# Unpacking of two 64-bit weights and placement of small copies in a fused attention, mixture and SoLU kernel

## The chip, the cores and the metric

The kernel runs on one core of one Trainium2 chip. The metric is the device time of one execution in microseconds. The engines of the core are TensorE (PE in the profile), VectorE (DVE), ScalarE (ACT), GpSimd (POOL) and SyncE (SP, which here only issues DMAs). Each engine works through its own instructions strictly in the order in which they stand; between engines they wait for semaphores.

## The reference

Three layers follow each other; what matters here is the last two.

```python
p_packed = sm_attn(p, k, v)              # 8 batches, 8 heads, 576 positions, 64 wide, 32 packed
x = sm_attn(q, p_packed, p_packed)       # -> x of 4608 x 512
logits = x @ phi                         # 32 slots = 8 experts x 4
d = softmax over tokens;  slot_input = d.T @ x
for e in range(8):
    h = np.maximum(slot_input[e] @ w1[e], 0.0)     # 512 -> 1024
    slot_out[e] = h @ w2[e]                        # 1024 -> 512
x = (softmax over slots) @ slot_out
h = x @ w_in                             # 512 -> 1024
solu = h * softmax(h);  ln = (solu - mean) / sqrt(var + 1e-6) * g_ln
out = ln @ w_out                         # 1024 -> 512
```

`w_in` and `w_out` arrive as 64-bit floats (a 32-bit array times a 64-bit scalar). [...]

## The kernel before

It has three stages on the chip, and a planner that orders the first two together and the third by itself.

**Stage 1, attention and routing (0 to about 128 us).** Eight batches in four pairs; K, Q, V are loaded into a ring of 14 tiles (`ring`, tile `r`). For each pair the packed attention, its softmax (tiles `A`, `bmx`, `bsum`), the transposes and the running softmax over tokens are made. Between these the planner puts the unpacking of `w_in` (tile `wif`), marked `soft`: only into gaps. Stage 1 ends with the slot inputs `SIT`.

**Stage 2, the experts (about 128 to 192 us).** The weights of the eight experts come in 29 loads of 9 pieces (`w12`) through the same ring. For expert e, `mk_w1` multiplies 16 pieces with `SIT` (L935), takes the ReLU into `hs` on ScalarE (L946), transposes it on TensorE (L951) and copies it out as `hT` (L955); `mk_w2` multiplies 16 pieces with `hT` (L976), copies the result to `so` on ScalarE (L991), transposes it (L995) and writes it, scaled and three times, into `SO` (L1000). A copy `hs` or `so` thus stands between two pieces of TensorE work. `sw` = `SO` x `w_in` (L1214) ends the stage.

Beside the experts `w_out` is unpacked in eight chunks of 128x512 (`mk_unpack`, with `wo_bound` and `wo_tail`):

- VectorE takes the exponent bits of the upper word into `ux` (L1077) and the mantissa bits into `ua` (L1080); ScalarE turns the exponent into that of a 32-bit float, in place in `ux` (L1087, a ReLU with the bias `ebias`).
- TensorE multiplies the power of two in `ux`, read as 16-bit numbers two apart, with `ga` and adds it up over the eight chunks (`wo_bound`, L1141): a bound from which the column scales `wsc` and `winv` come.
- VectorE adds the lower word to the mantissa (L1092) and, after the bound's multiplication has read `ux`, puts the sign bit onto `ux` (L1099). GpSimd multiplies `ua` by `ux` (L1152).

When all eight are done, ScalarE copies the bound (L1161), VectorE makes the scales in four steps (L1165 to L1178), and then for each chunk VectorE scales it (`q1`, L1188), ScalarE rounds it to 16 bits as `whi` (`q2`, L1193) and GpSimd subtracts this to get `wlo` (`q3`, L1196).

**Stage 3 (about 201 us to the end).** 36 tiles of 128 tokens: `h` (L1272), softmax and norm on VectorE, ScalarE and GpSimd, then 24 multiplications of 128x512 a tile with `whi` and `wlo` (L1392, L1398). In its steady part TensorE follows itself without a gap.

**What sets the order.** `Plan` lists each step with its engine, an estimated length, what it depends on, buffers it takes (`acq`) and gives back (`rel`) and an urgency, plays this through, and writes the instructions in the order of the start times that come out. Estimates only decide the order; on the chip an engine waits at its next instruction, whatever stands behind it. Idle places of TensorE are filled with multiplications of zeros (`wz`, L319).

Of the kernel before, what the change touches and what calls it, by code (L numbers as in the profile page):

```python
# [138 lines left out]
def pack_attention__soft_moe__solu_kernel(  # L139
# [55 lines left out]
    with ExitStack() as p12, tc.manual_schedule():  # L195
# [12 lines left out]

        phi_sb = at.tile([128, 4, 32], FP32, name="phi_sb", bufs=1)
        plan = Plan({"ring": RING, "ring2": 0, "sc": 2, "w": 4, "v": 0, "a": 4, "aT": 2, "grp": 5, "ST": 1, "A2": 2, "A2T": 1, "d": 1, "T": 1,  # L210
                     "h": 2, "u": 2, "c3": 1}, LOOK1, CALM1, REST1)
        now = [0]

        def op(*args, urgent=0, **kw):
# [712 lines left out]
        def mk_w1(e):  # L927
            def pe(g0, g1):
                def go():
                    if g0 == first(e):  # L930
                        ps_t["h", e] = bank()
                    hp = ps_t["h", e]
                    for i in range(g0, g1):
                        k, g = divmod(i - first(e), 4)
                        nc.tensor.matmul(  # L935
                            out=hp[32 * g:32 * g + 32, 0:256],
                            lhsT=SIT[:, k, :],
                            rhs=gran(i),
                            start=(k == 0),
                            stop=(k == 3),  # L940
                        )
                return go

            def act():
                hs = hs_t[e] = W["k"].tile([128, 256], FP32, tag="hs", name="hs")
                nc.scalar.activation(out=hs, in_=ps_t.pop(("h", e))[:, 0:256], func=ACTF.Relu)  # L946

            def tr():
                t = ps_t["ht", e] = bank()
                for j in range(2):  # L950
                    nc.tensor.transpose(t[:, 128 * j:128 * j + 128], hs_t[e][:, 128 * j:128 * j + 128], ident)  # L951

            def dve():
                hT = hT_t[e] = W["k"].tile([128, 2, 4, 32], FP32, tag="hT", name="hT")
                nc.vector.tensor_copy(  # L955
                    hT, ps_t.pop(("ht", e))[:, 0:256].rearrange("p (j g s) -> p j g s", j=2, g=4)
                )

            x = stream(first(e), first(e) + 16, pe, 95, [o_2, o_w1.get(e - 1)], ["w", "h"], [])
            o_w1[e] = x  # L960
            x = op("ACT", 264, act, [x], rel=["w"])
            x = op("PE", 214, tr, [x], acq=["w"])
            o_hT[e] = op("ACT" if 0 else "DVE", 330, dve, [x], rel=["w"], urgent=10 ** 5)

        def mk_w2(e):
            def pe(g0, g1):
# [18 lines left out]
            def tail(h0, h1, dep):  # L985
# [11 lines left out]
                def dve():  # L997
# [12 lines left out]
            s0, s1 = second(e), second(e) + 16  # L1010
            o = [o_hT[e], o_w2.get(e - 1)]
# [52 lines left out]
        def mk_unpack(key, c, tail, deps, between=None):  # L1064
            def words():
                raw = loaded[key][:, 1024 * c:1024 * c + 1024].bitcast(UINT32).rearrange("p (n w) -> p n w", w=2)
                return raw[:, :, 0], raw[:, :, 1]

            def dve():
                lo, hi = words()  # L1070
                if key[0] == "wi":
                    a = wif[:, key[1], 512 * c:512 * c + 512]
                else:
                    a = W["k"].tile([128, 512], FP32, tag="ua", name="ua")
                ua_t[key, c] = a
# [29 lines left out]
            x = op("DVE", ns[0], dve, deps, acq=["u"], soft=so)  # L1105
            y = op("ACT", ns[1], act, [x], soft=so)
            z = op("DVE", ns[2], dve2, [x], soft=so)
            ys = [y, between(2 * key[1] + c, key, c, y)] if between else [y]
            z = op("DVE", ns[3], dve3, ys + [z], rel=["ring"] if key[0] == "wi" and c == 1 else [], soft=so)
            return tail(key, c, z)  # L1110

        def wi_tail(key, c, z):
            def pool():
                a, x = ua_t.pop((key, c)), ux_t.pop((key, c))
                nc.gpsimd.tensor_tensor(out=a, in0=a, in1=x.bitcast(FP32), op=ALU.mult)

            return op("Pool", 1225, pool, [z], rel=["u"], soft=True)

# [18 lines left out]
        def wo_bound(k, key, c, dep):  # L1137
            def pe():
                if k == 0:
                    ps_t["bd"] = bank2()  # L1140
                nc.tensor.matmul(  # L1141
                    out=ps_t["bd"], lhsT=W["ga"][:, k, :], rhs=ux_t[key, c].bitcast(BF16).rearrange("p (n w) -> p n w", w=2)[:, :, 1],
                    start=(k == 0), stop=(k == 7),
                )

            o_bd.append(op("PE", 220, pe, [dep, o_ga] + o_bd[-1:], acq=["v"] if k == 0 else [], urgent=10 ** 5))
            return o_bd[-1]

# [37 lines left out]
        for k in range(8):  # L1186
# [11 lines left out]
            y = op("DVE", 1100, q1, [x, o_wo[k]])  # L1198
# [355 lines left out]
```

## Time and profile before

| | us |
|---|---|
| three runs | 417.67, 419.58, 419.73 |
| median | 419.58 |
| the profiled execution | 419.56 |
| its span | 417.7 |
| busy in it: PE, DVE, ACT, POOL | 393.2, 280.3, 231.5, 197.6 |

A row of the profile gives start or busy time, engine, line of the kernel, the tile that is written and those that are read, shape and count. In brackets stands the idle time of the engine before the row and what ended it. A multiplication of 32-bit floats on TensorE stands as two records.

### The profile page before, as it was taken

How to read it: one execution, taken by the hardware profiler on the slowest of the kernel's cores; microseconds unless marked ns; L12 is line 12 of the kernel's file. 1: busy time of each engine (PE TensorE's matmuls, PEld its weight loads, DVE VectorE, ACT ScalarE, POOL GpSimd, SP SyncE). 2: the span in 40 equal slices, each digit the busy share in tenths (PEclk: the TensorE clock that was granted, in tenths of full speed). 3: DMA queues.
4: the chain of work that ended last, by engine and by line, in shares of the span. 5: the costliest groups of instructions: out<-in, count | busy, mean ns of one | idle time of the engine just before them, and what ended most of it. 6: DMA issues, size and time to landing. Idle time of an engine off the chain costs nothing.

```text
span 417.7 us, 9713 instructions
## 1 busy us (share of the span) xinstructions
PE 393.2 (94%) x3807; PEld 210.6 (50%) x3807; DVE 280.3 (67%) x587; ACT 231.5 (55%) x430; POOL 197.6 (47%) x296
## 2 busy tenths in 40 slices
PE   8989999998799999879879999999999999999997
PEld 3455565655445777544334444444444444444445
DVE  2177889988956465880896666667666767766641
ACT  1357777867444334240588556665566556666530
POOL 1033545351610222291179665666665666656650
PEclk9999999999999999998999999999999999999999
DMA  8999999999999999900037756776756867668662
GB/s 305 414 418 407 416 412 414 415 418 412 417 423 376 391 375 423 385 4 0 0 52 168 171 117 126 140 163 137 136 121 136 154 137 127 146 124 148 151 142 86
DMA packets 91149, 99.27 MB, mean 238 GB/s; under 512 B 76128, under 2 KB 76640, under 8 KB 85472
## 3 DMA queue, kind: packets, MB, share of 16 engines
q1 hardware_dynamic: 90816, 98.58, 73.9%
q8 instruction: 30, 0.49, 0.5%
q14 instruction: 15, 0.12, 0.1%
q10 hardware_dynamic: 288, 0.07, 0.1%
HBM read 70.85 MB, written 9.44 MB: 192 GB/s over the span
## 4 chain that ended last, share of the span: by engine, by line
PE 74%; DVE 13%; DMA 7%; issue 2%; ACT 2%; POOL 1%; SPq 1%; ACTq 0%; DVEq 0%; POOLq 0%
PE o L1392 28%; PE o L1398 14%; PE w L976 5%; PE w L935 4%; PE h L1272 3%; DMA r<-kT 3%; DMA r<-qT 3%; PE sc L335 2%; DVE r L1188 2%; PE w L418 2%; PE sw L1214 2%; PE w L319 2%; DVE bmx L507 2%; PE w L575 1%; PE o L1405 1%
## 5 line engine op out<-in xcount | busy, mean ns | idle before, releaser
L1392 PE MATMUL o<-whi,th 128*128 128x512 f16 x280 | 106.1, 379 | 1.7 <-DMA th<-hi 1.3
L1392 PE MATMUL o<-wlo,th 128*128 128x512 f16 x280 | 106.1, 379 | 0.0
L1362 POOL TENSOR_TENSOR lo<-x,hi 128x1024 f16<-128x1024 f32 (+1 forms) x37 | 77.4, 2093 | 29.5 <-ACT hi L1355 29.5
L1392 PEld LDWEIGHTS <-th 128*128 128x128 f16 x560 | 54.6, 98 | 67.7 <-DMA th<-hi 1.7
L1398 PE MATMUL o<-whi,tl 128*128 128x512 f16 x280 | 66.5, 380 | 0.0
L1321 ACT ACTIVATE e<-s3t,nv 128x1024 f32<-128x1024 f32 x36 | 41.3, 1148 | 43.9 <-DVE nmean L1315 43.9
L1355 ACT ACTIVATE hi<-s3t,nr,rs 128x1024 f16<-128x1024 f32 (+1 forms) x37 | 44.9, 1217 | 25.4 <-POOL nr L1342 25.4
L1302 DVE SCALAR_TENSOR_TENSOR s3t<-h,e 128x1024 f32<-128x1024 f32 (+1 forms) x37 | 44.0, 1191 | 20.2 <-ACT e L1293 20.2
L1347 DVE TENSOR_SCALAR x<-s3t,nmean,rs 128x1024 f32<-128x1024 f32 (+1 forms) x37 | 30.1, 816 | 35.6 <-POOL rs L1338 35.6
L1280 DVE TENSOR_REDUCE nm<-h 128x1 f32<-128x1024 f32 (+1 forms) x37 | 43.9, 1188 | 2.5 <-PE h L1272 2.4
L1398 PEld LDWEIGHTS <-tl 128*128 128x128 f16 x280 | 24.9, 98 | 34.3 <-issue 8.6
L1293 ACT ACTIVATE e<-h,nm 128x1024 f32<-128x1024 f32 (+1 forms) x37 | 39.7, 1074 | 3.4 <-DVE nm L1285 2.9
L976 PE MATMUL w<-r,hT 128*32 128x128 f32 x512 | 30.8, 284 | 0.2 <-DVE hT L955 0.2
L319 PE MATMUL w<-wz 128*128 128x512 f16 x105 | 29.5, 380 | 1.6 <-ACT bq L446 0.5
L1272 PE MATMUL h<-swr,cT 96*128 96x512 f32 x72 | 28.7, 483 | 1.6 <-DVE swr L1226 1.4
L1152 POOL TENSOR_TENSOR r<-ua,ux 128x512 f32<-128x512 f32 x8 | 10.7, 1336 | 38.3 <-DVE ux L1099 38.3
L1420 DVE TENSOR_TENSOR ob<-o,winv 128x512 f32<-128x512 f32 x35 | 24.0, 684 | 5.8 <-PE o L1398 5.8
L976 PEld LDWEIGHTS w<-r,hT 128*32 128x32 f32 x512 | 25.7, 113 | 4.0 <-issue 1.9
L539 POOL TENSOR_TENSOR A<-A,bsum 128x512 f32<-128x512 f32 (+1 forms) x18 | 19.0, 1061 | 18.5 <-DVE bsum L531 11.6
L935 PE MATMUL w<-r,SIT 128*32 128x256 f32 x256 | 22.6, 384 | 0.0
L1338 POOL TENSOR_TENSOR rs<-rs,half 128x1 f32<-128x1 f32 x36 | 20.1, 558 | 2.8
L1337 POOL TENSOR_TENSOR rs<-V,w 128x1 f32<-128x1 f32 x36 | 7.4, 206 | 27.9 <-ACT e L1321 27.9
(187 smaller groups left out, 614.9 us busy)
## 6 DMA issues: line engine op xcount, KB each, us to landing
r<-w SPq DMA_DIRECT2D x28, 1152.0 KB, 11.2
r<-kT SPq DMA_DIRECT2D x16, 576.0 KB, 13.4
r<-v SPq DMA_DIRECT2D x8, 1152.0 KB, 14.1
r<-qT SPq DMA_DIRECT2D x16, 576.0 KB, 14.7
out<-ob SPq DMA_DIRECT2D x31, 256.0 KB, 2.3
r<-w_in SPq DMA_DIRECT2D x4, 1024.0 KB, 14.2
r<-w_out SPq DMA_DIRECT2D x4, 1024.0 KB, 20.5
out<-ob SPq DMA_DIRECT2D x16, 64.0 KB, 1.7
```

The lines of the kernel that those rows point to most:

```text
L319: nc.tensor.matmul(out=t[:, 0:FN], lhsT=wz[:, 0:128], rhs=wz[:, 0:FN], start=True, stop=True)
L935: nc.tensor.matmul(out=hp[32 * g:32 * g + 32, 0:256], lhsT=SIT[:, k, :], rhs=gran(i), start=(k == 0), stop=(k == 3),)
L976: nc.tensor.matmul(out=sp[32 * k:32 * k + 32, 0:128], lhsT=hT_t[e][:, j, g, :], rhs=gran(i)[:, 128 * c:128 * c + 128], start=(f == 0), sto ...
L1272: nc.tensor.matmul(out=w, lhsT=cT[:, t, :], rhs=swr[n], start=True, stop=True)
L1280: nc.vector.tensor_reduce(out=z["nm"][:, h:h + 1], in_=hcols(h), axis=AX.X, op=ALU.max, negate=True)
L1293: nc.scalar.activation(out=z["e"][:, cols(h)], in_=hcols(h), func=ACTF.Exp, bias=z["nm"][:, 0:1], accum_out=z["S"][:, h:h + 1],)
L1302: nc.vector.scalar_tensor_tensor(out=z["s"][:, cols(h)], in0=hcols(h), scalar=1.0, in1=z["e"][:, cols(h)], op0=ALU.mult, op1=ALU.mult, acc ...
L1321: nc.scalar.activation(out=z["e"], in_=z["s"], func=ACTF.Square, bias=z["nv"], scale=2.0 ** -15, accum_out=z["V"])
L1355: nc.scalar.activation(out=z["hi"][:, cols(h)], in_=z["s"][:, cols(h)], func=ACTF.Identity, scale=z["r"], bias=z["nr"])
L1362: nc.gpsimd.tensor_tensor(out=z["lo"][:, cols(h)], in0=z["x"][:, cols(h)], in1=z["hi"][:, cols(h)], op=ALU.subtract)
L1392: nc.tensor.matmul(out=z["o"], lhsT=z["th"][:, c, :], rhs=w[:, c, :], start=(c == 0 and w is whi), stop=False)
L1398: nc.tensor.matmul(out=z["o"], lhsT=z["tl"][:, c, :], rhs=whi[:, c, :], start=False, stop=(c == 7))
```

## The change

The sign now goes onto the mantissa `ua`, not onto the power of two `ux`. So `ux` is never written again after ScalarE, is kept as 16-bit numbers (the bits of a bf16), and the sign step waits neither for ScalarE nor for the bound's multiplication; GpSimd's product waits for both. For `w_out`, `ux` has four buffers of its own, given back by the bound's multiplication. The two copies of an expert that VectorE made, `hT` and `SO`, go to ScalarE; rounding to `whi` goes from ScalarE to GpSimd. Some estimated lengths change with it.

```diff
-        nc.gpsimd.memset(ebias, -896.0 * 2.0 ** 23)
+        nc.gpsimd.memset(ebias, -896.0 * 2.0 ** 7)
...
-            def dve():
+            def act2():
                 hT = hT_t[e] = W["k"].tile([128, 2, 4, 32], FP32, tag="hT", name="hT")
-                nc.vector.tensor_copy(
+                nc.scalar.copy(
...
-            o_hT[e] = op("ACT" if 0 else "DVE", 330, dve, [x], rel=["w"], urgent=10 ** 5)
+            o_hT[e] = op("ACT", 330, act2, [x], rel=["w"], urgent=10 ** 5)
...
-                    nc.vector.tensor_scalar(
-                        out=W["SO"][:, 2 * h0:2 * h1, :, 4 * e:4 * e + 4],
-                        in0=src[:, :, None, :].broadcast_to([128, n, 3, 4]),
-                        scalar1=2.0 ** -52, scalar2=None, op0=ALU.mult,
+                    nc.scalar.mul(
+                        W["SO"][:, 2 * h0:2 * h1, :, 4 * e:4 * e + 4],
+                        src[:, :, None, :].broadcast_to([128, n, 3, 4]), 2.0 ** -52,
                     )
...
-                o_SOT[e, h1 - 1] = op("DVE", 200, dve, [x], rel=["w"], urgent=10 ** 5)
+                o_SOT[e, h1 - 1] = op("ACT", 250, act2, [x], rel=["w"], urgent=10 ** 5)
...
+            def top():
+                raw = loaded[key][:, 1024 * c:1024 * c + 1024].bitcast(UINT16).rearrange("p (n w) -> p n w", w=4)
+                return raw[:, :, 3]
...
-                x = ux_t[key, c] = uk.tile([128, 512], UINT32, tag="ux", name="ux")
+                pool = uk if key[0] == "wi" else W["k"]
+                x = ux_t[key, c] = pool.tile([128, 512], UINT16, tag="ux", name="ux", bufs=2 if key[0] == "wi" else 4)
                 nc.vector.tensor_scalar(
-                    out=x, in0=hi, scalar1=20, scalar2=0x7FF, op0=ALU.logical_shift_right, op1=ALU.bitwise_and
+                    out=x, in0=top(), scalar1=4, scalar2=0x7FF, op0=ALU.logical_shift_right, op1=ALU.bitwise_and
                 )
...
-                nc.scalar.activation(out=x, in_=x, func=ACTF.Relu, scale=2.0 ** 23, bias=ebias)
+                nc.scalar.activation(out=x, in_=x, func=ACTF.Relu, scale=2.0 ** 7, bias=ebias)
...
-                x = ux_t[key, c]
+                a = ua_t[key, c].bitcast(UINT32)
                 nc.vector.scalar_tensor_tensor(
-                    out=x, in0=hi, scalar=0x80000000, in1=x, op0=ALU.bitwise_and, op1=ALU.bitwise_or
+                    out=a, in0=hi, scalar=0x80000000, in1=a, op0=ALU.bitwise_and, op1=ALU.bitwise_or
                 )
...
-            ys = [y, between(2 * key[1] + c, key, c, y)] if between else [y]
-            z = op("DVE", ns[3], dve3, ys + [z], rel=["ring"] if key[0] == "wi" and c == 1 else [], soft=so)
-            return tail(key, c, z)
+            if between:
+                between(2 * key[1] + c, key, c, y)
+            z = op("DVE", ns[3], dve3, [z], rel=["ring"] if key[0] == "wi" and c == 1 else [], soft=so)
+            return tail(key, c, [y, z])
...
-                nc.gpsimd.tensor_tensor(out=wo_chunk(2 * key[1] + c), in0=a, in1=x.bitcast(FP32), op=ALU.mult)
+                nc.gpsimd.tensor_tensor(out=wo_chunk(2 * key[1] + c), in0=a, in1=x.bitcast(BF16), op=ALU.mult)
...
             def q2(k=k):
-                nc.scalar.copy(W["hi"][:, k, :], wo_chunk(k))
+                nc.gpsimd.tensor_copy(W["hi"][:, k, :], wo_chunk(k))
...
-            y = op("ACT", 620, q2, [y, o_3])
+            y = op("Pool", 700, q2, [y, o_3])
```

The order that comes out moves at three places. On ScalarE at the end of stage 2, from the copy of the bound to `sw` (`whi` is the rounded weight, `hs`, `hT`, `so` and `SO` belong to the experts), there stands before:

```order
L1161 COPY winv<-v 128x512
L1193 CAST whi<-r 128x512
L991 COPY so<-w 128x128
L1193 CAST whi<-r 128x512 x3
L946 ACTIVATE hs<-w 128x256
L1193 CAST whi<-r 128x512 x4
L991 COPY so<-w 128x128
L991 COPY so<-w 64x128 x2
L1222 CAST swr_2349<-sw 96x512
```

and now:

```order
L1166 COPY winv<-v 128x512
L1001 ACTIVATE SO<-w 128x12x4
L947 ACTIVATE hs<-w 128x256
L956 COPY hT<-w 128x256
L992 COPY so<-w 128x128
L1001 ACTIVATE SO<-w 128x12x4
L947 ACTIVATE hs<-w 128x256
L956 COPY hT<-w 128x256
L992 COPY so<-w 128x128
L1001 ACTIVATE SO<-w 128x12x4
L992 COPY so<-w 64x128
```

The eight roundings have left; only steps of the experts remain, and each of them waits for TensorE. On GpSimd the eight subtractions now have eight roundings among them, from the first on.

On TensorE the tail of stage 2, from the last eight pieces of expert 7's first layer (`SIT`) on, reads before:

```order
L935 MATMUL w<-r,SIT 32x256 x8
L976 MATMUL w<-r,hT 32x128 x2
L319 LDWEIGHTS wz
L319 MATMUL w<-wz 128x512
L951 MATMUL w<-ident,hs 128x128 x2
L976 MATMUL w<-r,hT 32x128 x18
L319 LDWEIGHTS wz
```

and now:

```order
L936 MATMUL w<-r,SIT 32x256 x8
L977 MATMUL w<-r,hT 32x128 x2
L952 MATMUL w<-ident,hs 128x128 x2
L320 LDWEIGHTS wz
L320 MATMUL w<-wz 128x512
L977 MATMUL w<-r,hT 32x128 x18
L320 LDWEIGHTS wz
```

One filler has moved behind the transposes of `hs`; all that follows up to `sw` is as it was. Farther ahead, the last multiplication of the bound has moved from behind twelve `hT` multiplications of load 21 to in front of expert 4's `so` transpose, and one more filler stands behind that transpose (nine in the stage, not eight).

On VectorE, in the last pair of stage 1, the two sign steps of a piece of `w_in` stood together ahead of the maxima `bmx` of the last pair's softmax:

```order
L531 TENSOR_SCALAR bsum<-bsum 128x16
L535 RECIPROCAL bsum<-bsum 128x16
L1099 SCALAR_TENSOR_TENSOR ux<-r,ux 128x512 x2
L507 TENSOR_REDUCE bmx<-w 128x16
L662 STREAM_TRANSPOSE lt<-ls 128x32
```

and now one of them does,

```order
L532 TENSOR_SCALAR bsum<-bsum 128x16
L536 RECIPROCAL bsum<-bsum 128x16
L1104 SCALAR_TENSOR_TENSOR wif<-r,wif 128x512
L508 TENSOR_REDUCE bmx<-w 128x16
L663 STREAM_TRANSPOSE lt<-ls 128x32
```

while the other stands earlier, behind the addition of the lower word and ahead of `pb`, a copy that takes a product of TensorE:

```order
L1097 SCALAR_TENSOR_TENSOR wif<-wif,r 128x512
L1104 SCALAR_TENSOR_TENSOR wif<-r,wif 128x512
L430 TENSOR_SCALAR pb<-w,r 128x64
L508 TENSOR_REDUCE bmx<-w 128x16
L515 TENSOR_TENSOR A_1893<-w,bmx 128x512
```

In stage 2 too the sign steps, which stood behind ScalarE and the bound, now stand one or two rows behind that addition.

The rest of stage 1 and all of stage 3 stand in the same order as before on every engine.

## Rows read from the trace of the kernel before

**Rows 1.** Busy time by stage: window, length, engines, clock, DMA.

```profile
128.00:175.90 47.90, 47.70 (x691) 33.40 (x691) 29.98 (x58) 17.76 (x38) 10.65 (x8) 1.00 0.98 394
175.90:192.00 16.10, 10.98 (x154) 7.66 (x154) 10.39 (x13) 5.72 (x12) 11.66 (x8) 0.89 0.07 26
218.60:417.70 199.10, 196.09 (x924) 93.50 (x924) 128.37 (x229) 116.69 (x163) 121.58 (x197) 1.00 0.67 138
```

**Rows 2.** TensorE in order of time, 174 to 197 us: start, duration, operation.

```profile
174.86 1.03 PE L935 MATMUL w<-r,SIT 128*32 128x256 f32 x14
177.65 0.33 PE L995 MATMUL w<-ident,so 128*128 128x128 f32 x1 [1.76 <-ACT so L991]
177.82 0.38 PE L319 MATMUL w<-wz 128*128 128x512 f16 x1
178.13 1.07 PE L935 MATMUL w<-r,SIT 128*32 128x256 f32 x16
179.02 0.39 PE L976 MATMUL w<-r,hT 128*32 128x128 f32 x4
...
180.67 0.44 PE L951 MATMUL w<-ident,hs 128*128 128x128 f32 x2 [0.94 <-ACT hs L946]
181.03 1.76 PE L976 MATMUL w<-r,hT 128*32 128x128 f32 x36
...
183.05 1.76 PE L976 MATMUL w<-r,hT 128*32 128x128 f32 x36
186.81 0.33 PE L995 MATMUL w<-ident,so 128*128 128x128 f32 x1 [2.00 <-ACT so L991]
...
187.28 2.95 PE L976 MATMUL w<-r,hT 128*32 128x128 f32 x36
190.65 0.37 PE L995 MATMUL w<-ident,so 64*128 64x64 f32 x1 [0.41 <-ACT so L991]
...
191.96 3.67 PE L1214 MATMUL sw<-wif,SO 128*96 128x512 f32 x8
```

**Rows 3.** ScalarE in order of time, 169 to 187 us.

```profile
169.66 0.72 ACT L1087 ACTIVATE ux<-ux,ebias 128x512 uint32<-128x512 uint32 x1 [1.72 <-DVE ux L1077]
...
176.82 0.62 ACT L1193 CAST whi<-r 128x512 f16<-128x512 f32 x1 [3.94 <-DMA r<-w]
177.34 0.26 ACT L991 COPY so<-w 128x128 f32<-128x128 f32 x1
...
180.24 0.38 ACT L946 ACTIVATE hs<-w 128x256 f32<-128x256 f32 x1
```

**Rows 4.** One line each: durations in ns (least/median/most), first and last start.

```profile
L1188 DVE SCALAR_TENSOR_TENSOR r<-r,g_sb,wsc x8: 744/1422/1645, 176.0 to 184.3; 128x512 f32<-128x512 f32 x8
...
L1196 POOL TENSOR_TENSOR wlo<-r,whi x8: 1147/1600/1617, 177.5 to 188.0; 128x512 f16<-128x512 f32 x8
...
L1077 DVE TENSOR_SCALAR ux<-r x16: 365/419/1255, 28.9 to 169.2; 128x512 uint32<-128x512 uint32 x16
...
L1099 DVE SCALAR_TENSOR_TENSOR ux<-r,ux x16: 628/692/1533, 34.5 to 172.3; 128x512 uint32<-128x512 uint32 x16
```

**Rows 5.** VectorE and TensorE in order of time, 97 to 107 us.

```profile
98.50 0.28 DVE L429 TENSOR_SCALAR pb<-w,r 128x64 f32<-128x64 f32 x1 [0.80 <-PE w L418]
...
104.41 2.08 DVE L1099 SCALAR_TENSOR_TENSOR ux<-r,ux 128x512 uint32<-128x512 uint32 x2
...
105.26 0.66 PE L495 MATMUL w<-ident,ST 128*128 128x128 f32 x4
```

**Rows 6.** GpSimd: the rounding it makes (groups by form), and its first step of stage 3.

```profile
L231 POOL CAST ident<-ident 128x128 f16<-128x128 f32 x1 | 0.3, 290 | 0.1
...
204.81 0.19 POOL L1329 TENSOR_TENSOR S<-S 128x1 f32<-128x1 f32 x1 [15.64 <-ACT e L1293]
```

**Rows 7.** TensorE in order of time, 168 to 172 us.

```profile
168.00 0.33 PE L995 MATMUL w<-ident,so 128*128 128x128 f32 x1
...
171.85 0.40 PE L1141 MATMUL v<-ux,ga 128*128 128x512 bf16 x1
```

More of the change, by code (lines that the diff above doesn't have):

```diff
@@ L12 @@
 BF16 = mybir.dt.bfloat16
+UINT16 = mybir.dt.uint16
 UINT32 = mybir.dt.uint32
@@ L210, in pack_attention__soft_moe__solu_kernel @@
         plan = Plan({"ring": RING, "ring2": 0, "sc": 2, "w": 4, "v": 0, "a": 4, "aT": 2, "grp": 5, "ST": 1, "A2": 2, "A2T": 1, "d": 1, "T": 1,
-                     "h": 2, "u": 2, "c3": 1}, LOOK1, CALM1, REST1)
+                     "h": 2, "u": 2, "x": 4, "c3": 1}, LOOK1, CALM1, REST1)
         now = [0]
@@ L995, in tr, with act2 @@
                     nc.tensor.transpose(t[:, r], so_t[e][r], ident[r, r])
-                def dve():
+                def act2():
                     src = ps_t.pop(("st", e))[:, r].rearrange("p (c s) -> p c s", s=32)[:, :, 4 * e:4 * e + 4]
                     n = 2 * (h1 - h0)
-                    nc.vector.tensor_scalar(
-                        out=W["SO"][:, 2 * h0:2 * h1, :, 4 * e:4 * e + 4],
-                        in0=src[:, :, None, :].broadcast_to([128, n, 3, 4]),
-                        scalar1=2.0 ** -52, scalar2=None, op0=ALU.mult,
+                    nc.scalar.mul(
+                        W["SO"][:, 2 * h0:2 * h1, :, 4 * e:4 * e + 4],
+                        src[:, :, None, :].broadcast_to([128, n, 3, 4]), 2.0 ** -52,
                     )
@@ L1104, in mk_unpack @@
             ns = (670, 613, 602, 602) if so else (1100, 720, 740, 1000)
-            x = op("DVE", ns[0], dve, deps, acq=["u"], soft=so)
+            x = op("DVE", ns[0], dve, deps, acq=["u"] if so else ["u", "x"], soft=so)
             y = op("ACT", ns[1], act, [x], soft=so)
             z = op("DVE", ns[2], dve2, [x], soft=so)
-            ys = [y, between(2 * key[1] + c, key, c, y)] if between else [y]
-            z = op("DVE", ns[3], dve3, ys + [z], rel=["ring"] if key[0] == "wi" and c == 1 else [], soft=so)
-            return tail(key, c, z)
+            if between:
+                between(2 * key[1] + c, key, c, y)
+            z = op("DVE", ns[3], dve3, [z], rel=["ring"] if key[0] == "wi" and c == 1 else [], soft=so)
+            return tail(key, c, [y, z])
         def wi_tail(key, c, z):
@@ L1114, in pool @@
                 a, x = ua_t.pop((key, c)), ux_t.pop((key, c))
-                nc.gpsimd.tensor_tensor(out=a, in0=a, in1=x.bitcast(FP32), op=ALU.mult)
-            return op("Pool", 1225, pool, [z], rel=["u"], soft=True)
+                nc.gpsimd.tensor_tensor(out=a, in0=a, in1=x.bitcast(BF16), op=ALU.mult)
+            return op("Pool", 1225, pool, z, rel=["u"], soft=True)
         def wo_chunk(k):
@@ L1141, in pe @@
                 nc.tensor.matmul(
-                    out=ps_t["bd"], lhsT=W["ga"][:, k, :], rhs=ux_t[key, c].bitcast(BF16).rearrange("p (n w) -> p n w", w=2)[:, :, 1],
-                    start=(k == 0), stop=(k == 7),
+                    out=ps_t["bd"], lhsT=W["ga"][:, k, :], rhs=ux_t[key, c].bitcast(BF16), start=(k == 0), stop=(k == 7)
                 )
-            o_bd.append(op("PE", 220, pe, [dep, o_ga] + o_bd[-1:], acq=["v"] if k == 0 else [], urgent=10 ** 5))
+            o_bd.append(op("PE", 220, pe, [dep, o_ga] + o_bd[-1:], acq=["v"] if k == 0 else [], rel=["x"], urgent=10 ** 5))
             return o_bd[-1]
@@ L1150, in pool @@
             def pool():
-                a, x = ua_t.pop((key, c)), ux_t.pop((key, c))
-                nc.gpsimd.tensor_tensor(out=wo_chunk(2 * key[1] + c), in0=a, in1=x.bitcast(FP32), op=ALU.mult)
-            return op("Pool", 1330, pool, [z], rel=["u"])
+                a, x = ua_t.pop((key, c)), ux_t[key, c]
+                nc.gpsimd.tensor_tensor(out=wo_chunk(2 * key[1] + c), in0=a, in1=x.bitcast(BF16), op=ALU.mult)
+            return op("Pool", 1330, pool, z, rel=["u"])
         for i in range(4):
@@ L1192, in q2 @@
             def q2(k=k):
-                nc.scalar.copy(W["hi"][:, k, :], wo_chunk(k))
+                nc.gpsimd.tensor_copy(W["hi"][:, k, :], wo_chunk(k))
             def q3(k=k):
                 nc.gpsimd.tensor_tensor(out=W["lo"][:, k, :], in0=wo_chunk(k), in1=W["hi"][:, k, :], op=ALU.subtract)
-            y = op("DVE", 1100, q1, [x, o_wo[k]])
-            y = op("ACT", 620, q2, [y, o_3])
+            y = op("DVE", 1300, q1, [x, o_wo[k]])
+            y = op("Pool", 700, q2, [y, o_3])
             y = op("Pool", 1400, q3, [y], rel=["ring"] if k % 2 else [])
```

## The prediction, made before the changed kernel ran

> **What bounds the kernel now.** I read the busy time by stage first. In the experts' steady part TensorE is busy 47.70 of 47.90 us; VectorE (29.98), ScalarE (17.76) and GpSimd (10.65) have room. From 218.6 us to the end TensorE is busy 196.09 of 199.10 us at clock 1.00. Between these, from 175.9 to 192.0 us, it is busy only 10.98 of 16.10 us and its granted clock is 0.89 [rows 1]. Stage 3 follows `sw`, and its length is TensorE's own, so what brings `sw` forward brings the end forward by as much. That stretch is the first question.
>
> TensorE in order of time names what it waits for there: `so`, `hs`, `so` and `so`, all from ScalarE, 1.76, 0.94, 2.00 and 0.41 us [rows 2]. ScalarE is not busy then; it stands. At 176.82 it ends an idle time of 3.94 us with the first rounding to `whi`, and the copy `so`, whose input was ready, comes only behind it at 177.34 [rows 3]. The rounding waited for `q1` on VectorE, which begins at 176.0 [rows 4]; the name of a DMA in that bracket is only the event that came last in the record. So copies of the experts stand in line behind roundings that wait for a slow chain: `q1` takes 744 ns at best but 1422 in the middle, and GpSimd's subtraction 1147 at best but 1600 in the middle [rows 4], since the two are slow when they lie beside each other.
>
> **The change part by part.**
>
> *The roundings leave ScalarE.* On ScalarE's new order only experts' steps follow the copy of the bound, so I replay TensorE's tail with its own durations. Fourteen `SIT` records stand before the stop at 174.86; sixteen take 179.02 - 178.13 = 0.89 us, so fourteen take 0.78 and the transposition of `so` starts at 175.64, not 177.65 (-2.01). It and the filler take 178.13 - 177.65 = 0.48: the last sixteen start at 176.12 and end, by their 1.07, at 177.19. ScalarE then makes `hs`: 0.38 and about 0.05 us on either side, so the transpositions start at 177.67, not 180.67 (-3.00). Two transpositions take 181.03 - 180.67 = 0.36, and the filler that now stands behind them 0.32: `hT` x36 starts at 178.35, not 181.03 (-2.68). The next chunk came 183.05 - 181.03 = 2.02 later, a filler included, so 180.37; after 1.71 more it is done, at 182.08. ScalarE copies `so` (0.26, and 0.05 on either side); its transposition starts near 182.2, not 186.81 (-4.6), and the last 36 pieces at 182.67, not 187.28. [rows 2, 3]
>
> These last 36 took 2.95 us, where the same 36 took 1.76 before [rows 2]. That is the lower granted clock: 0.89 on the mean of the stretch [rows 1], so a part of it at 1.2 and not 2.4 GHz, and it came behind the idle times of 1.76, 0.94 and 2.00. In the new order the longest idle time left is about 0.5, so I take 1.76. The last copy is ready at 184.79 instead of 190.65. From there to `sw` it took 1.31 at the lower clock; I take 0.29 for the transposition and 16/36 x 1.71 = 0.76 for the pieces beside it. `sw` starts at 185.84, not 191.96: -6.12. [rows 2]
>
> *`hT` and `SO` go to ScalarE.* `hs`, of the size of `hT`, takes 0.38 there [rows 3]. A copy costs about the same as on VectorE, and ScalarE has 30 us free in the steady part [rows 1]; the price is the queue: `hT` and `SO` now stand behind the ReLUs of `ux`. I count 0.1 for the last `SO`, which is on the path, and nothing for the rest, because TensorE works on the other expert's pieces meanwhile. The ninth filler of the stage costs 0.3 (as the one from 177.82 to 178.13 [rows 2]).
>
> *The 16-bit `ux`.* Reading one 16-bit word of four and writing half as much is in no row. The step takes 419 ns in the middle now [rows 4]; I bound it by half of that, 210, and by the 692 of a step with two inputs, and take 420. Sixteen such steps lie on VectorE, eight of them in stage 2 where it has 18 us free.
>
> *The sign on `ua`.* It takes 692 as before [rows 4]: two inputs, the same size. In the last pair of stage 1 two sign steps held VectorE from 104.41 for 2.08 us; the maxima behind them had to wait until 106.49 [rows 5]. Now one stands there, ending near 105.1 or a little later, but the maxima also need TensorE's transposition of `ST`, from 105.26 for 0.66: they start at 105.96, not 106.49, so -0.5. The other sign step falls into VectorE's idle 0.80 before 98.50 [rows 5] and fits with its 0.69. Bounds: 0 (the step does not fit, or the loads, busy 0.98 of the next stage [rows 1], hold the start) to -1.4, a whole step. I take -0.4.
>
> *GpSimd gets eight roundings.* A 128x512 rounding there is in no row; four times the 128x128 one of 290 ns [rows 6] is 1.16, the subtraction of the same size 1.15 at its best and 1.60 in the middle [rows 4]. From below the 0.29 of the quarter bounds it, from above 1.60; less than nothing is excluded, since it is work that GpSimd did not have. I take 1.15, on which two rows agree. With 1.15 for the subtraction and some 0.45 lost where `q1` lies beside them (1600 - 1147), eight chunks take 22 us. The chain starts sooner: the last multiplication of the bound, at 171.85, now stands in front of the transposition of 168.00 [rows 7], and `q1` came 4.15 behind it [rows 4, 7], so from 172.2 at the latest; GpSimd ends near 194. Stage 3 asks for GpSimd at 204.81 [rows 6], which becomes 198.7: about 4 us of cover, and the roundings cost nothing. If the cover is gone, each microsecond counts in full.
>
> The Trainium skill speaks against this part. In *SBUF — State Buffer*, "Who interferes with whom", it states that a VectorE operation with two inputs in SBUF and a GpSimd operation reading SBUF exclude each other for the whole instruction. Our trace agrees in kind, with `q1` at 744 alone and up to 1645 beside GpSimd; by that rule roundings, too, would alternate with `q1`, and the third rival below prices this. In *GPSIMD Engine Reference*, "3.1 Elementwise — side-by-side cycle accounting", a one-input loop over 512 elements is given with 769 ns; by that, as an estimate, the eight chunks take 19 us and not 22. No row here shows it.
>
> **The sum.** -6.12 (tail) + 0.1 (`SO`) + 0.3 (filler) - 0.4 (attention) = -6.1. No moved step issues a DMA, and transfers end 7% of 16.1 = 1.1 us into the tail [rows 1], so no queue is passed. Against the profiled execution's 419.56 that gives 413.4; the median of the runs, 419.58, is the same. Half a per cent, 2.1 us, is about what a measurement of this kernel can tell from no change.
>
> **Rivals.**
>
> 1. *The clock falls anyway.* The waits left, 0.5 for `hs` and for `so`, could still pull it down. Against it: from 128 to 175.9 the experts hand over through the same copies and the clock is 1.00 [rows 1]. Price 2.95 - 1.76 = 1.2, and 0.2 in what follows: 414.8.
>
> 2. *VectorE's and ScalarE's new steps hold TensorE in stage 2.* ScalarE idled 1.72 us for `ux` at 169.66 [rows 3]; were the bound later instead of earlier, or a copy late once or twice at the end, half the gain would go: 416.5. Against it is all the free time of [rows 1].
>
> 3. *The GpSimd chain decides.* If `q1` starts at 176.0 as now and rounding takes the 1600 of the subtraction, eight times (1.6 + 1.6) from 176.8 end at 202.4, 3.7 behind the 198.7 at which stage 3 asks: 417.1. Against it are the bound's earlier place [rows 7] and casting with one input.
>
> 4. *Nothing is gained.* The waits for `so` and `hs` only change their name (`hT` on ScalarE in place of `whi`): 419.5. Against it: an expert's steps depend only on TensorE.
>
> 5. *Slower.* `hT` now stands on ScalarE behind the ReLU of `ux`, and that waits for VectorE, as at 169.66 for 1.72 us [rows 3]. Each expert has one such ReLU in its time. When the stall passes what TensorE has in store, it is paid eight times; from 6.1/8 = 0.77 us each the gain is gone, and at 1.0 us each the time is 413.4 + 8 = 421.4. For it: `hT` was on an engine with no such wait; against it: the first copy waits only as long as VectorE is late, and `ux` now needs no bound's multiplication before the sign.
>
> **How the numbers follow.** Forecast 0.63 (its own range 411.8 to 415.0: attention 1.0 to either side, 0.6 for gaps in the tail), rival 1 0.12, rival 2 0.08, rival 3 0.08, rival 4 0.05, rival 5 0.04. Faster by over 0.5% means below 417.5: the forecast and rivals 1 to 3 but for a few hundredths of the third, 0.88; within it rival 4 and those hundredths, 0.08; slower 0.04. The range is 411.0 (all of the 1.4 in attention, and a fast `ux`) to 417.0; it leaves out rivals 4 and 5 and part of 3.
>
> **What would show it.** Right: from 174 to 186 us no wait of TensorE for `so` or `hs` above 0.6 us, clock 1.00 there, `sw` near 185.5; GpSimd done by 195 and stage 3's first step there near 198.5, not the other way round; the maxima of the last pair 0.5 earlier; stage 3 as long as now. Wrong: TensorE waiting for `hT` (rival 5), `o` waiting for `wlo` (rival 3), the last 36 pieces at nearly 3 us (rival 1), or `sw` early while the first tiles of stage 3 are not.

## The result and the profile after

The changed kernel takes 413.35 us (median of 4 runs, 412.80 to 413.46) against 418.74 in runs of the kernel before on the same chip; the ratio is 0.987, with a 95% interval from 0.984 to 0.990. The forecast was 413.4 us, with a range from 411.0 to 417.0. The span of the profiled executions went from 417.7 to 411.6 us. The four runs before lie in two groups, 417.67 and 417.90, 419.58 and 419.73, and the profiled one, 419.56 at a mean granted clock of 0.996, belongs to the upper. Times below are medians of all runs; the ratios are not formed from these medians and can differ from theirs by up to 0.2 per cent.

Busy time by stage in the changed kernel, in the columns of [rows 1]; its last window is as long as the last one there and begins as much sooner as the span is shorter:

```profile
128.00:175.90 47.90, 47.90 (x688) 32.29 (x680) 31.02 (x49) 20.84 (x52) 13.26 (x11) 1.00 0.99 397
175.90:192.00 16.10, 14.88 (x166) 8.81 (x166) 4.52 (x4) 2.22 (x9) 13.35 (x14) 1.00 0.05 17
212.50:411.60 199.10, 195.73 (x924) 93.58 (x924) 128.29 (x229) 116.71 (x163) 121.55 (x197) 1.00 0.67 139
```

In the tail TensorE is busy 14.88 of 16.10 us, not 10.98, at clock 1.00, not 0.89; as `sw` starts sooner, these 16.10 us now also hold 6.1 us of what stood behind them. Stage 3 has kept its length: from the start of `sw` to the end of the span it is 225.74 us before and 225.71 now. The tail on TensorE, against [rows 2]:

```profile
174.45 1.03 PE L936 MATMUL w<-r,SIT 128*32 128x256 f32 x14
175.42 0.33 PE L996 MATMUL w<-ident,so 128*128 128x128 f32 x1
...
175.89 1.07 PE L936 MATMUL w<-r,SIT 128*32 128x256 f32 x16
...
177.53 0.44 PE L952 MATMUL w<-ident,hs 128*128 128x128 f32 x2 [0.36 <-ACT hs L947]
...
178.11 1.76 PE L977 MATMUL w<-r,hT 128*32 128x128 f32 x36
...
182.04 0.33 PE L996 MATMUL w<-ident,so 128*128 128x128 f32 x1 [0.17 <-ACT so L992]
...
182.52 1.76 PE L977 MATMUL w<-r,hT 128*32 128x128 f32 x36
184.69 0.27 PE L996 MATMUL w<-ident,so 64*128 64x64 f32 x1 [0.41 <-ACT so L992]
...
185.89 3.67 PE L1219 MATMUL sw<-wif,SO 128*96 128x512 f32 x8
```

The waits of 1.76, 0.94 and 2.00 us are gone or down to 0.36 and 0.17; the last 36 pieces take 1.76 and not 2.95; `sw` starts at 185.89 instead of 191.96, which is 6.07 of the 6.1 us by which the span is shorter. ScalarE, against [rows 3], now waits for TensorE alone:

```profile
174.67 0.27 ACT L992 COPY so<-w 128x128 f32<-128x128 f32 x1 [2.14 <-PE w L977]
...
177.09 0.38 ACT L947 ACTIVATE hs<-w 128x256 f32<-128x256 f32 x1 [1.10 <-PE w L936]
```

What GpSimd has taken over, its durations and VectorE's beside them (one line each, as [rows 4]), and GpSimd in order of time (as [rows 6]):

```profile
L1198 POOL CAST whi<-r x8: 608/1038/1073, 172.7 to 183.1; 128x512 f16<-128x512 f32 x8
...
L1201 POOL TENSOR_TENSOR wlo<-r,whi x8: 1150/1153/1592, 173.8 to 188.1; 128x512 f16<-128x512 f32 x8
...
L1193 DVE SCALAR_TENSOR_TENSOR r<-r,g_sb,wsc x8: 744/1092/1650, 171.8 to 179.3; 128x512 f32<-128x512 f32 x8
...
L1082 DVE TENSOR_SCALAR ux<-r x16: 361/419/1255, 28.4 to 160.8; 128x512 uint16<-128x512 uint16 x16
```

```profile
183.65 5.60 POOL L1201 TENSOR_TENSOR wlo<-r,whi 128x512 f16<-128x512 f32 x5
198.74 0.19 POOL L1334 TENSOR_TENSOR S<-S 128x1 f32<-128x1 f32 x1 [9.49 <-ACT e L1298]
```

GpSimd ends at 183.65 + 5.60 = 189.25 and stands 9.49 us until stage 3 asks for it at 198.74.

### The profile page after: what moved, and what is told of

Same layout as the page of the kernel before. It is cut to its first block, busy times and chain, and to the rows that moved or that the text cites. A ratio compares the mean times of both kernels' runs of the same rounds, so it can differ in the third digit from the quotient of the medians.

```text
span 411.6 us, 9721 instructions
## 1 busy us (share of the span) xinstructions
PE 391.5 (95%) x3808; PEld 208.7 (51%) x3808; DVE 274.7 (67%) x570; ACT 231.1 (56%) x439; POOL 199.9 (49%) x304
## 4 chain that ended last, share of the span: by engine, by line
PE 77%; DVE 9%; DMA 7%; ACT 2%; issue 2%; POOL 1%; SPq 1%; ACTq 0%; DVEq 0%; POOLq 0%
PE o L1397 29%; PE o L1403 14%; PE w L977 6%; PE w L936 5%; PE h L1277 3%; DMA r<-kT 3%; DMA r<-qT 3%; PE sc L336 2%; PE w L320 2%; PE w L419 2%; PE sw L1219 2%; DVE bmx L508 2%; PE w L576 1%; PE o L1410 1%; PE w L379 1%
## 5 line engine op out<-in xcount | busy, mean ns | idle before, releaser
L977 PE MATMUL w<-r,hT 128*32 128x128 f32 x512 | 28.8, 275 | 0.0
L977 PEld LDWEIGHTS w<-r,hT 128*32 128x32 f32 x512 | 24.1, 109 | 3.0 <-issue 2.2
L540 POOL TENSOR_TENSOR A<-A,bsum 128x512 f32<-128x512 f32 (+1 forms) x18 | 18.1, 1017 | 13.7 <-DVE bsum L532 6.9
```

Of the source, the lines that this page charges most:

```text
L977: nc.tensor.matmul(out=sp[32 * k:32 * k + 32, 0:128], lhsT=hT_t[e][:, j, g, :], rhs=gran(i)[:, 128 * c:128 * c + 128], start=(f == 0), sto ...
```

## The experiments

Two theories stood against each other. Q: the copies of the experts stood in ScalarE's queue behind roundings that wait for `q1`, and taking the roundings out of that queue is the whole gain. P: the gain comes from VectorE's relief and from a chain of `q1` that starts sooner. Later runs ask what the other parts of the change are worth, how long GpSimd's cover is, and whether the multiplications of zeros hold the clock. Ratios are to the kernel before, with their 95% interval.

### The rounding alone moved

To the kernel before:

```
-                nc.scalar.copy(W["hi"][:, k, :], wo_chunk(k))
+                nc.gpsimd.tensor_copy(W["hi"][:, k, :], wo_chunk(k))
...
-            y = op("DVE", 1100, q1, [x, o_wo[k]])
-            y = op("ACT", 620, q2, [y, o_3])
+            y = op("DVE", 1300, q1, [x, o_wo[k]])
+            y = op("Pool", 700, q2, [y, o_3])
```

> The kernel before with one step moved: the rounding to whi goes from ScalarE to GpSimd; signs, 32-bit ux, hT and SO stay. Theory Q (the experts' copies stood in ScalarE's queue behind roundings that wait for q1): TensorE's waits for so and hs between 175 and 188 us go, sw comes near 187, and the time is 414.6 us (413.35 of the changed kernel + 0.67 for the attention, whose first SIT moved by that much, - 0.3 for a filler, + 0 to 2.5 because hT of expert 7 stands behind five q1 on VectorE, of which I take 0.9). Theory P (the gain comes from VectorE's relief and from q1 starting four us sooner): q1 still starts at 176, so the time stays at 417.5 or above.

Measured: 413.74 us, ratio 0.989 [0.986, 0.991]. VectorE and TensorE in order of time:

```profile
175.54 1.41 DVE L1188 SCALAR_TENSOR_TENSOR r<-r,g_sb,wsc 128x512 f32<-128x512 f32 x2
...
185.80 3.67 PE L1214 MATMUL sw<-wif,SO 128*96 128x512 f32 x8
```

`q1` starts at 175.54, nearly as late as before, and `sw` comes at 185.80 all the same. One edit, with the order that the planner makes of it (the filler again stands behind the transposes of `hs`), carries the gain: Q holds and P falls. The size was 0.9 us too high: that was charged for `hT` of expert 7 behind five `q1`, and TensorE does not wait for it here.

### The rounding back on ScalarE

To the changed kernel, with TensorE's order the same row by row:

```
-                nc.gpsimd.tensor_copy(W["hi"][:, k, :], wo_chunk(k))
+                nc.scalar.copy(W["hi"][:, k, :], wo_chunk(k))
...
-            y = op("DVE", 1300, q1, [x, o_wo[k]])
-            y = op("Pool", 700, q2, [y, o_3])
+            y = op("DVE", 1100, q1, [x, o_wo[k]])
+            y = op("ACT", 620, q2, [y, o_3])
```

> The changed kernel with the rounding to whi back on ScalarE; all else as changed, TensorE's order the same row by row. Theory Q: five roundings stand before so of expert 6 and eight before hs of expert 7; with q1 from 171.8 at 1.08 to 1.42 us each, hs of expert 7 comes at 181.0 to 183.8 instead of 177.1, the clock falls again (+1.2), and the time is 417.4 to 421.3, say 419.5 us. Theory P: q1 is early (172) and that is what counts, so the time is below 415.

Measured: 420.64 us, ratio 1.0045 [1.0026, 1.0064], slower than before. VectorE's `q1`, ScalarE's last rounding ahead of `hs`, TensorE, and the window of the tail:

```profile
171.49 9.89 DVE L1193 SCALAR_TENSOR_TENSOR r<-r,g_sb,wsc 128x512 f32<-128x512 f32 x8
...
181.42 0.62 ACT L1198 CAST whi<-r 128x512 f16<-128x512 f32 x1 [0.94 <-DVE r L1193]
181.94 0.38 ACT L947 ACTIVATE hs<-w 128x256 f32<-128x256 f32 x1
...
177.57 0.33 PE L996 MATMUL w<-ident,so 128*128 128x128 f32 x1 [2.41 <-ACT so L992]
...
182.38 0.69 PE L952 MATMUL w<-ident,hs 128*128 128x128 f32 x2 [2.71 <-ACT hs L947]
...
183.42 2.80 PE L977 MATMUL w<-r,hT 128*32 128x128 f32 x36
```

```profile
175.90:192.00 16.10, 11.14 (x151) 7.68 (x153) 5.49 (x4) 4.33 (x12) 8.72 (x7) 0.79 0.01 5
```

`q1` starts at 171.5 here, four us sooner than in the run above, and yet the time is 7 us longer: an early chain is no help when the experts' copies stand behind it. The clock fell too: from the first `SIT` to `sw` this kernel takes 65.32 us and the changed one 58.64, and of these 6.68 the waits for `so` and `hs` are 4.76 (2.41 + 2.71, less the 0.36 that is left in the changed kernel). The other 1.9 go with the lower clock, at which 36 pieces take 2.80 and not 1.76.

### The signs and the 16 bits alone

To the changed kernel: the edit of the last experiment, and `hT` and `SO` on VectorE as before, by

```
-                nc.scalar.copy(
+                nc.vector.tensor_copy(
...
-            o_hT[e] = op("ACT", 330, act2, [x], rel=["w"], urgent=10 ** 5)
+            o_hT[e] = op("DVE", 330, act2, [x], rel=["w"], urgent=10 ** 5)
...
-                o_SOT[e, h1 - 1] = op("ACT", 250, act2, [x], rel=["w"], urgent=10 ** 5)
+                o_SOT[e, h1 - 1] = op("DVE", 200, act2, [x], rel=["w"], urgent=10 ** 5)
```

> The kernel before with the sign on the mantissa and the 16-bit ux, but with hT and SO on VectorE and the roundings on ScalarE. Theory Q: only the attention's 0.67 us is gained, 418.1 us against 418.74, and TensorE waits for so and hs as before. Theory P: the signs bring the chain of q1 forward and half of the gain is there, 416.5 or less.

Measured: 417.01 us, ratio 0.9967 [0.9951, 0.9983]: 1.4 us where 0.7 was expected. ScalarE's first rounding, TensorE's waits, and the window of the tail:

```profile
175.06 0.62 ACT L1199 CAST whi<-r 128x512 f16<-128x512 f32 x1 [3.31 <-DVE r L1194]
...
175.90 0.33 PE L996 MATMUL w<-ident,so 128*128 128x128 f32 x1 [1.13 <-ACT so L992]
...
178.92 0.44 PE L952 MATMUL w<-ident,hs 128*128 128x128 f32 x2 [1.27 <-ACT hs L947]
...
185.05 0.33 PE L996 MATMUL w<-ident,so 128*128 128x128 f32 x1 [1.78 <-ACT so L992]
...
185.53 1.76 PE L977 MATMUL w<-r,hT 128*32 128x128 f32 x36
```

```profile
175.90:192.00 16.10, 12.63 (x161) 7.95 (x161) 8.67 (x10) 5.14 (x11) 11.53 (x8) 1.00 0.04 14
```

The waits for `so` and `hs` are there, as Q says. The expectation's size failed. The first rounding is at 175.06, not 176.82 [rows 3]: 1.03 of that is the start of stage 2 (first `SIT` at 126.89, not 127.92), and some 0.6 the last sign step, which no longer stands between the bound's multiplication and the scales (`q1` starts 3.54 behind that multiplication, not 4.18). And the clock stayed at 1.00, so the last 36 took 1.76. Its span, 415.0, is 2.7 shorter than that of the profiled execution before; the median 1.4. All eleven runs have a mean clock of 0.998 or more; that the shorter waits did this is likely, but not shown.

### The placement alone

The kernel before with `hT` and `SO` on ScalarE and the rounding on GpSimd, with the old sign step and 32 bits (the diffs above and in the change).

> The kernel before with hT and SO on ScalarE and the rounding on GpSimd, but the old sign step on ux and ux in 32 bits. Theory Q: all of the tail's gain without the attention's, 414.0 us. Rival S (the format matters in stage 2, since ux then waits for the bound's multiplication before the sign and holds VectorE): TensorE waits in stage 2 and the time is 415.5 or above.

Measured: 414.18 us, ratio 0.989 [0.987, 0.992], as Q forecast. The format of `ux` holds nothing up in stage 2: from the first `SIT` to the fourteen it takes 47.28 us, in the changed kernel 47.20.

### `hT` and `SO` back on VectorE

The changed kernel with the second diff of the signs' experiment alone.

> The changed kernel with hT and SO back on VectorE; signs, 16-bit ux and rounding on GpSimd as changed. Theory Q (the roundings' place alone carries the tail): no wait for so above 0.3 us comes back, one filler less stands in stage 2 (-0.3), hT of expert 7 stands behind five q1 and still arrives by 181, so 413.1 us (412.7 to 413.7). Rival (hT and SO behind q1 on VectorE stop TensorE): waits for hT of a microsecond each in the tail, 414.5 us or above.

Measured: 413.37 us, ratio 0.989 [0.988, 0.991]: within its expectation, and the same as the changed kernel. Moving `hT` and `SO` is worth nothing here; what it does to the order (a ninth filler, 0.3 us) is as small as forecast.

### The rounding on ScalarE, but last

```
-                nc.gpsimd.tensor_copy(W["hi"][:, k, :], wo_chunk(k))
+                nc.scalar.copy(W["hi"][:, k, :], wo_chunk(k))
...
-            y = op("DVE", 1300, q1, [x, o_wo[k]])
-            y = op("Pool", 700, q2, [y, o_3])
+            y = op("DVE", 1100, q1, [x, o_wo[k]])
+            y = op("ACT", 620, q2, [y, o_3, o_SOT[NE - 1, 0]])
```

> The changed kernel with the rounding to whi back on ScalarE, but placed behind the copies so of expert 7 instead of between those of experts 6 and 7. Theory Q (the place in ScalarE's queue, not the engine, costs the time): sw's first half starts at 186 as now, six roundings end by 190 and shift SO's last part by 0 to 0.4, wlo ends near 197 before stage 3 asks at 198.7, so 413.5 us (413.2 to 414.5). Rival E (ScalarE is the wrong engine for it wherever it stands, or GpSimd's later chain decides): 416 us or above.

Measured: 413.85 us, ratio 0.990 [0.989, 0.992]. VectorE's `q1` in one line, then ScalarE and GpSimd in order of time:

```profile
L1193 DVE SCALAR_TENSOR_TENSOR r<-r,g_sb,wsc x8: 742/742/752, 172.1 to 176.7; 128x512 f32<-128x512 f32 x8
...
186.25 0.26 ACT L992 COPY so<-w 64x128 f32<-64x128 f32 x1 [0.30 <-PE w L977]
186.54 2.70 ACT L1198 CAST whi<-r 128x512 f16<-128x512 f32 x5
...
186.02 9.04 POOL L1201 TENSOR_TENSOR wlo<-r,whi 128x512 f16<-128x512 f32 x8 [15.21 <-ACT whi L1198]
198.98 0.19 POOL L1334 TENSOR_TENSOR S<-S 128x1 f32<-128x1 f32 x1 [3.92 <-ACT e L1298]
```

On the engine on which it cost 7 us, the rounding costs about 0.5 when it stands behind the experts' copies, and none of that up to `sw`: from the first `SIT` it takes 58.65 us, as in the changed kernel (58.64). The place in the queue is the cause, not the engine. A `q1`, with nothing on GpSimd beside it, takes 742 ns in the middle, where it took 1092 in the changed kernel.

### More roundings on GpSimd

Each rounding made twice, and in another kernel four times:

```
-                nc.gpsimd.tensor_copy(W["hi"][:, k, :], wo_chunk(k))
+                for _ in range(2): nc.gpsimd.tensor_copy(W["hi"][:, k, :], wo_chunk(k))
```

> The changed kernel with each of the eight roundings on GpSimd made twice. GpSimd is done at 189.3 now and has 9.5 us until stage 3 asks for it. Eight more of 0.57 (alone) to 1.04 us (beside q1) end it at 194 to 197.5. Theory H (the roundings are hidden): 413.4 us, no change. Rival G (GpSimd's chain already sets the first tiles of stage 3): each of these microseconds counts, 417.5 us or above.

> The changed kernel with each of the eight roundings on GpSimd made four times. Twice cost nothing and ended GpSimd at 193.8 instead of 189.3. Sixteen more of 0.61 end it at 203 to 204, 4 to 5 us behind the 198.7 at which stage 3 asks for GpSimd. Theory G (the cover is what the trace shows as idle time, and beyond it each microsecond counts): 417.5 to 418.5 us. Rival (the first tiles have more room than that idle time): below 416 us.

Measured: twice 413.65 us (0.992 [0.989, 0.995]), four times 418.40 (1.000 [0.998, 1.002]). GpSimd in the first of them, then GpSimd and TensorE in the second:

```profile
188.17 5.60 POOL L1201 TENSOR_TENSOR wlo<-r,whi 128x512 f16<-128x512 f32 x5
198.19 0.19 POOL L1334 TENSOR_TENSOR S<-S 128x1 f32<-128x1 f32 x1 [4.42 <-ACT e L1298]
```

```profile
199.44 5.62 POOL L1201 TENSOR_TENSOR wlo<-r,whi 128x512 f16<-128x512 f32 x5
205.02 0.19 POOL L1334 TENSOR_TENSOR S<-S 128x1 f32<-128x1 f32 x1
...
208.29 1.31 PE L1382 MATMUL tr<-ident,hi 128*128 128x128 f16 x8 [4.19 <-ACT hi L1360]
```

Half of the idle 9.49 us used up costs nothing in the median (413.65); of the seven runs, though, three took 414.64, 415.79 and 418.00, the last two with a mean clock of 0.996, and why is open. With four times, GpSimd ends at 205.06, where 203 to 204 was expected. That moves stage 3's first step there from 198.74 to 205.02, 6.3 us, TensorE's transposition of `hi` from 203.37 to 208.29, 4.9 us, and the time by 5.1. The last of these is not the chain alone: behind the wait of 4.19 the clock fell to 0.50 from 208 to 214 us, and a later wait of TensorE for a transfer, 1.56 us in the changed kernel, is gone. So beyond the cover the price comes out nearly one for one, as the third rival of the prediction had it, but with other terms in it.

### Without the multiplications of zeros

The changed kernel; then the same with `hT` and `SO` on VectorE; then the kernel before:

```
-                    if not sw_t:
+                    if not sw_t and "k" not in W:
```

> The changed kernel without the nine multiplications of zeros in stage 2 and its tail; everything else in the same order. They stand on TensorE's path with 0.31 us each. Theory C1 (the clock fell in the kernel before because of idle times near 2 us; single waits of 0.4 do not lower it): clock 1.00 stays, and the time falls by the fillers that no wait takes over, 1.0 to 2.8 us, to 411.5. Rival C2 (the fillers hold the clock): the granted clock of 176 to 192 falls below 0.95 and the time is 414.5 or above.

Measured: 409.82 us, ratio 0.981 [0.979, 0.982], the fastest of all. TensorE, and the tail's window:

```profile
182.76 3.67 PE L1219 MATMUL sw<-wif,SO 128*96 128x512 f32 x8
```

```profile
175.90:192.00 16.10, 13.85 (x144) 7.96 (x138) 5.61 (x6) 2.82 (x9) 13.05 (x14) 1.00 0.03 11
```

The clock stays at 1.00: in the changed kernel C2 falls, and C1's forecast of the clock holds. `sw` is 3.13 us sooner, where nine fillers by 0.31 are 2.8. They had filled no wait; they stood on the path. The time falls by 3.5, more than the 2.8 that the expectation had as the most: 0.1 is the start of stage 2, and 0.4 comes behind `sw`, where nothing was changed and where the profiled executions with the same stage 3 (all but the one with four roundings) differ among themselves, from 224.9 to 226.2 us.

> The changed kernel without the multiplications of zeros in stage 2 and with hT and SO back on VectorE. With fillers that place of hT and SO was worth nothing (413.37 against 413.35). Theory H (TensorE's order alone counts): 409.8 us again, 409.5 to 410.1. Rival (without fillers TensorE is earlier by 3 us, while q1 on VectorE is not, so hT of expert 7 comes too late behind q1): 410.8 us or above, with a wait for hT in the tail.

Measured: 412.26 us, ratio 0.985 [0.984, 0.987]. The rival was right:

```profile
179.64 0.41 DVE L956 COPY hT<-w 128x256 f32<-128x256 f32 x1
...
180.10 0.85 PE L977 MATMUL w<-r,hT 128*32 128x128 f32 x12 [1.19 <-DVE hT L956]
```

`hT` of expert 7 comes out behind five `q1`, at 179.64, and TensorE now waits for it. With fillers it came just in time. So `hT` and `SO` on ScalarE, worth nothing in the change, are worth 2.4 us without fillers. `sw` comes 1.75 later, at 184.51: 1.19 are this wait, 0.15 the start of stage 2, and 0.41 lie between, where the order differs too; what is left comes behind `sw`.

> The kernel before without the eight multiplications of zeros in stage 2. Theory Q (its tail is set by q1 and the roundings in ScalarE's queue): only the two fillers ahead of the bound's last multiplication count, 0.6 us, the rest turns into longer waits for so and hs; 417.3 to 418.5 us. Rival F (the fillers cost their 0.31 each whatever waits there are): 415.5 us or below.

Measured: 416.12 us, ratio 0.995 [0.993, 0.997], between the two forecasts. ScalarE, TensorE and the tail's window:

```profile
175.78 0.62 ACT L1193 CAST whi<-r 128x512 f16<-128x512 f32 x1 [4.22 <-DVE r L1188]
...
176.62 0.33 PE L995 MATMUL w<-ident,so 128*128 128x128 f32 x1 [2.70 <-ACT so L991]
...
186.02 1.76 PE L976 MATMUL w<-r,hT 128*32 128x128 f32 x36
```

```profile
175.90:192.00 16.10, 13.88 (x155) 9.31 (x156) 9.38 (x11) 5.86 (x13) 11.66 (x8) 0.79 0.09 36
```

The chain of roundings is 1.04 sooner than in [rows 3], the two fillers ahead of it and 0.4 from stage 1, and the other fillers in front of the last roundings did turn into waits. I had missed two things: the filler behind the last full `so` is on the path, and where in the tail the clock is low changes. Here it fell earlier, behind the wait of 2.70 (0.79 in the window), and was back for the last 36 pieces, which took 1.76 and not 2.95. All eleven runs have a mean clock of 0.991 or 0.992, while those of the kernel before have 0.995 to 1.000. So where long waits remain, C2 cannot be ruled out: without the fillers the clock was lower in every run, though the time was shorter.

## Why the prediction was right

**The tail.** -6.12 was forecast and `sw` moved by 6.07, from 191.96 to 185.89 (forecast 185.84). The stops came in the forecast's order and near its times: `hs`'s transpositions at 177.53 (177.67), the transposition of `so` at 182.04 (182.2), the last 36 pieces at 182.52 (182.67). That the numbers agree so closely is in part luck. The fourteen `SIT` already start 0.41 sooner, which the replay left to the other terms; from there to `sw` the kernel before takes 17.10 us and the changed one 11.44, so the tail itself gave 5.66, 0.46 less than forecast. The fourteen took 0.97 and not 0.78, and from the last copy to `sw` it took 1.20 and not 1.05. The replay also has a slip: by its own terms the transposition of `so` starts at 182.08 + 0.36 = 182.44, not near 182.2. Attention and filler, forecast at -0.4 + 0.3, gave -0.41 in the profiled execution and made up for most of this.

That the roundings in ScalarE's queue are the cause is shown from both sides: they alone moved give 413.74, they alone put back 420.64, and put back behind the copies 413.85.

**The clock.** It stayed at 1.00, as forecast; rival 1 did not come. But of the 5.66 us 1.31 are a fall of the clock in the profiled execution before (from the last 36 pieces to `sw` 4.68 us there, 3.37 now), and that fall is not in every execution. Of the 56 runs of the kernel before that stand beside the experiments, 22 have a mean clock of 0.995 or 0.996, as the profiled one, and a median of 419.27 us; 34 have 0.999 or 1.000 and 417.96. The prediction worked from the former. Against the latter the change gains 4.6 us and not 6.1, and the median of 418.74 lies between the two. Why the clock falls in some runs of one kernel and not in others no run shows.

**`hT` and `SO`.** 0.4 was charged for them, and put back they change nothing that can be measured. From the first `SIT` to the fourteen at 174.45 the changed kernel takes 174.45 - 127.25 = 47.20 us, the kernel before 174.86 - 127.92 = 46.94: the forecast filler. The 0.1 for the last `SO` did not come: the second half of `sw` starts 4.16 us behind the first in both. The first `SIT` before and now:

```profile
127.92 1.27 PE L935 MATMUL w<-r,SIT 128*32 128x256 f32 x17
...
127.25 1.48 PE L936 MATMUL w<-r,SIT 128*32 128x256 f32 x18
```

In stage 2 TensorE nowhere waits for `hT` on ScalarE; rival 5 did not come.

**The attention.** -0.4 was forecast. The maxima of the last pair come 0.57 sooner, from 106.41 behind the two sign steps [rows 5] to 105.84, where they wait for the transposition as forecast. Before, then now:

```profile
106.41 0.68 DVE L507 TENSOR_REDUCE bmx<-w 128x16 f32<-128x512 f32 x1
...
104.30 0.63 DVE L1104 SCALAR_TENSOR_TENSOR wif<-r,wif 128x512 uint32<-128x512 uint32 x1
105.84 0.69 DVE L508 TENSOR_REDUCE bmx<-w 128x16 f32<-128x512 f32 x1 [0.92 <-PE w L496]
```

The first `SIT` came between 126.7 and 127.5 us in nine executions with the new sign step and between 127.4 and 127.9 in four with the old one; the mean difference is 0.5, though the two ranges overlap a little. In time, two pairs of kernels that differ in the signs and `ux` alone are 0.8 apart (414.18 and 413.35) and 0.4 apart (413.74 and 413.37).

**The 16 bits.** The step on VectorE takes 419 ns in the middle, as before. That was the value taken between the bounds.

**GpSimd.** Free of charge, as forecast; its sizes were off on the safe side. The rounding takes 608 ns alone and 1038 beside `q1`, where 1.15 was taken; `q1` starts at 171.8 (forecast 172.2 at the latest) and takes 1092 in the middle, not 1422; the chain ends at 189.25 and not near 194. The cover is 9.5 us, not 4. By the Trainium skill, *SBUF — State Buffer*, "Who interferes with whom", a VectorE operation with two inputs in SBUF, as `q1` is, contends with a GpSimd operation that reads SBUF, and the ports that they share are locked by one of them. The traces agree in kind, with the rounding at 608 alone and 1038 beside `q1`, and `q1` at 742 alone and 1092 beside GpSimd; that they exclude each other for the whole instruction is not shown. By the Trainium skill, *GPSIMD Engine Reference*, "3.1 Elementwise — side-by-side cycle accounting", a tight loop over 512 elements takes 769 ns at best. For the rounding 608 was measured.

**What it did not see.** The prediction charged 0.3 for the ninth filler and took the other eight for granted. All nine lay on the path: without them `sw` came 3.1 us sooner and the time fell by 3.5, over half of what the change itself gave. Nor did it see that the execution from which it worked held a fall of the clock that most others do not have.

## What to carry to other kernels

When an engine that is idle most of the time ends the waits of the busiest one, look at what stands ahead in its queue: a step that waits for a slow chain must not stand in front of a short copy that the bottleneck needs, and moving it behind the copy does as well as another engine. Before work is given to an engine off the path, read from the trace when that engine is next asked for; the idle time in front of that step is the room there is. Filling work on the bottleneck is paid in full as soon as the waits it was to fill are gone. And before a gain is forecast from one profile, look at which of the kernel's runs that profile belongs to: here 1.3 of 6.1 us were a fall of the clock that only some runs have.

## What the runs showed of the hardware

- The granted clock of the tail was 1.00 after TensorE's waits of 1.13, 1.27 and 1.78 us (signs alone), 0.89 with 1.76, 0.94 and 2.00 (the kernel before), 0.79 with 2.41 and 2.71 (rounding back on ScalarE) and 0.79 with 2.70, 0.70 and 0.38 (the kernel before without fillers). Each is one execution: the kernel before kept a mean clock of 0.999 or 1.000 in 34 of 56 runs, so its waits do not always lower it. A fall from 2.4 to 1.2 GHz for a part of it made 36 pieces take 2.80 to 2.95 us instead of 1.76. Nine multiplications of zeros between the experts' steps made no difference to it in the changed kernel, 1.00 with and without; in the kernel before, the mean was 0.991 or 0.992 in all runs without its eight, and 0.995 to 1.000 with them.
- Taking a 16-bit word out of each 64-bit number costs VectorE as much as taking a 32-bit one: 419 ns for 128x512.
- A rounding of 128x512 to 16 bits takes GpSimd 608 ns alone and 1038 beside VectorE's two-input step, ScalarE 620. That two-input step takes 742 ns in the middle with GpSimd idle, and 1092 beside its roundings and subtractions.
